# A layout planner's table of costs, its thresholds per visit, and the order in which waits are listed

## The chip, the cores and the metric

The kernel runs on one core of one Trainium2 chip. The time is the device time of one launch in microseconds; for the kernel before it is the median of three runs. A profile of one further execution is shown; its times are that execution's own.

## The reference

Two attention blocks over the same input `x` (1 x 2048 x 640, 32 heads of 20) are mixed by a gate of one number per token. Block A is full softmax attention; block B looks at 8 earlier positions, two apart.

```python
def _A_ref(x, wqkv, wo):
    q, k, v = ...                       # x @ wqkv, 32 heads of 20
    p = _softmax(jnp.einsum("bhqd,bhkd->bhqk", q, k) * scale, axis=-1)
    o = jnp.einsum("bhqk,bhkd->bhqd", p, v)
    return o.reshape(B, S, D) @ wo

def _B_ref(x, wqkv, wo):
    W, dil = 8, 2
    idx = pos[:, None] - (jnp.arange(W) * dil)[None, :]
    logits = jnp.einsum("bhsd,bhswd->bhsw", q, kg) * scale   # masked where idx < 0
    o = jnp.einsum("bhsw,bhswd->bhsd", _softmax(logits), vg)
    return o.reshape(B, S, D) @ wo

g = _sigmoid((x * gate_w).sum(-1, keepdims=True))
return g * a + (1 - g) * b              # a = _A_ref(x, ...), b = _B_ref(x, ...)
```

Nearly all of the work is block A's: 32 heads x 2048 x 2048 scores, each through an exponential.

## The kernel before

**Units and tiles.** Block A's scores are cut into units: one head, 128 keys, 512 queries. There are 2048 units, in 32 groups (a quarter of the queries and four heads each; `GROUPS`). A *tile* `s` (a *visit* of the main loop) takes two or three units. `qk(s)` (L1511) issues one matmul per unit into one of two PSUM buffers `score[s % 2]` (L1524), `exp(s)` (L1544) is one ScalarE activation over all of the tile's columns into one of five buffers `ebuf[s % 5]` (L1547), and `pv_slot` with `pv` (L1556) accumulates the products with the values in `obank`, four heads side by side (L1592). A score buffer has room for three units, and its third bank also serves as one of the three side banks `BANKS`.

**Rides.** A two-unit tile may carry a third unit that ScalarE doesn't touch. Its scores go to the third bank, VectorE turns them into `uD` (L1537) by integer arithmetic on the bits of a bf16 number, and three more VectorE operations with added shifts make `eD` (L806). The exponential of that unit is then the weighted sum of these four approximations, taken by four accumulations into `obank`, the weights being in `vS` (L798, on GpSimd). Four rides share their keys and form a quad; an `eD` operation covers the quad at once.

**Side work.** Everything else is written as Python generators: the projections of q, k and v (`gen_qd`, `gen_kd`, `gen_v`), the gate (`gen_gate`), block B (`gen_bproj`, `gen_b`), the normalisation of a finished group (`gen_norm`), the output projection (`gen_fold`, `gen_prefold`). A generator yields a request such as `("pe", cost, ready)`, `("dve", ahead, ready)`, `("act", ready)` or `("bank",)`, and goes on to issue its tasks when `step` (L1150) grants it.

**The planner.** No order of instructions is written by hand but for the head (to the first tile) and the tail (after the last). While the program is being built, `_Sched.task` (L188) books each instruction on its engine: it starts when its engine is free and when each task it depends on has ended plus a latency (`LAT`), and lasts for a charged duration. `SWITCH` is charged on TensorE whenever row-tiled matmuls (scores) follow column-tiled ones or the reverse. From these booked times the loop at the end of `_build` decides, visit by visit, how the next tile is formed (`next_tile`, `wanted`), which accumulations go in (`pv_slot`), and how much side work may be issued before the next tile (`spend`, up to the end of the previous exponential plus `SLACK`). `filler` (L1599) adds matmuls that change nothing where TensorE's booked load over the last 2.3 us is under `FILL`. The times decide only the order within each engine's queue; on the chip, semaphores decide when things run.

**Thresholds.** `PLAN` maps a visit number to eighteen thresholds: two slacks, the tolerances for a third unit and for a ride (`XTOL`, `DWAIT`, `DIDLE`, `DIDLE2`, `DTIME`), priorities of rides and of block B, how far VectorE work is booked ahead (`DVE_AHEAD`, `DAHEAD`), boosts, `RFILL`, `FILL`, `HOLD` and `BOFF`. They hold until the next entry.

**Waits.** `emit` (L245) writes each engine's queue. In front of an instruction it lists one `wait_ge` per semaphore still to be waited for, in the order in which the awaited tasks were issued. As the program is built, the wait listed first is carried by the instruction itself; further ones stand ahead of it as semaphore instructions. An exponential from the sixth tile on has two: the older exponential that wrote the same `ebuf`, and its own score matmuls.

Of the kernel before, what the change touches and what calls it, by code (L numbers as in the profile page):

```python
# [5 lines left out]
FP32 = mybir.dt.float32  # L6
# [20 lines left out]
PADB = 16  # L27
SCALE = float(DH) ** -0.5
NEG = -1.0e9
TOK = 256  # L30
# [20 lines left out]
    0: ((0.3, 0.64), 0.31, 2.5, 2.5, 0.49, -1.34, -0.1, 11.8, 7.0, 8.15, 0.52, 0.47, 4.4, 4.0, 0.0, 0.71, 2, 0.0),  # L51
    10: ((0.3, 0.64), 0.31, 2.5, 2.5, 0.66, -1.34, -0.1, 11.8, 7.0, 8.15, 0.52, 0.47, 4.4, 4.0, 0.0, 0.71, 2, 0.0),
    20: ((0.3, 0.64), 0.31, 2.5, 2.5, 0.49, -1.34, -0.83, 11.8, 7.0, 8.15, 0.52, 0.47, 4.4, 4.08, 0.0, 0.71, 2, 0.0),
    30: ((0.32, 0.68), 0.31, 2.5, 5.5, 0.94, -1.34, -0.83, 11.8, 7.0, 7.65, 0.52, 0.47, 4.4, 5.28, 0.0, 0.73, 2, 0.0),
    40: ((0.32, 0.68), 0.3, 2.5, 5.5, 0.94, -1.34, -0.83, 11.8, 7.0, 8.82, 0.52, 0.47, 4.4, 5.28, 0.0, 0.73, 2, 1),
    50: ((0.32, 0.81), 0.3, 2.5, 5.5, 0.94, -1.34, -0.83, 11.8, 7.0, 8.82, 0.52, 0.47, 4.4, 5.28, 0.0, 0.73, 2, 1),
    60: ((0.32, 0.68), 0.31, 2.5, 5.5, 0.94, -1.34, -0.83, 11.8, 6.7, 7.65, 0.52, 0.64, 4.4, 4.34, 0.0, 0.73, 2, 0),
    70: ((0.32, 0.68), 0.3, 2.5, 5.5, 0.94, -1.5, -0.83, 11.8, 5.5, 8.82, 0.52, 0.47, 4.76, 5.28, 0.0, 0.73, 2, 1),
    80: ((0.29, 0.82), 0.3, 2.5, 5.5, 0.94, -1.34, -0.83, 11.8, 7.0, 8.82, 0.52, 0.47, 4.4, 5.28, 0.0, 0.73, 2, 1),
    90: ((0.29, 0.82), 0.06, 2.5, 6.6, 0.95, -1.34, -0.83, 11.59, 7.0, 8.82, 0.52, 0.47, 4.4, 5.28, 0.0, 0.73, 2, 0),  # L60
    100: ((0.32, 0.68), 0.31, 2.5, 5.5, 0.94, -1.34, -0.83, 11.8, 7.0, 7.03, 0.52, 0.47, 4.4, 4.3, 0.0, 0.69, 2, -3),
    110: ((0.32, 0.68), 0.31, 2.5, 5.5, 0.94, -1.49, -0.5, 11.8, 7.0, 6.64, 0.52, 0.47, 4.4, 4.3, 0.0, 0.66, 2, -3),
    120: ((0.32, 0.68), 0.31, 5.5, 5.5, 0.94, -1.15, -0.5, 9.67, 7.0, 6.64, 0.52, 0.47, 4.4, 3.98, 0.0, 0.66, 2, -3),
    130: ((0.32, 0.68), 0.31, 2.5, 5.5, 0.82, -1.6, -0.5, 11.8, 7.0, 6.64, 0.52, 0.44, 4.4, 4.54, 0.0, 0.66, 2, 0),
    160: ((0.31, 0.76), 0.33, 2.5, 1.0, 0.82, -1.6, -0.34, 11.8, 7.0, 6.64, 0.61, 0.44, 4.4, 4.12, 0.0, 0.66, 2, 0),
    180: ((0.31, 0.76), 0.28, 2.5, 1.0, 0.72, -1.6, -0.5, 11.8, 5.5, 6.64, 0.52, 0.44, 4.4, 3.94, 0.0, 0.66, 2, 0),
    190: ((0.31, 0.76), 0.28, 2.5, 5.5, 0.72, -1.6, -0.5, 11.8, 5.5, 6.64, 0.52, 0.59, 3.16, 3.94, 0.0, 0.66, 2, 0),
    200: ((0.32, 0.68), 0.38, 2.5, 2.5, 0.94, -1.48, -0.65, 14.9, 7.0, 6.07, 0.52, 0.47, 4.4, 5.28, 0.0, 0.73, 1, -3),
    210: ((0.29, 0.69), 0.31, 2.5, 5.5, 0.94, -1.49, -0.5, 11.8, 7.0, 7.54, 0.67, 0.62, 4.4, 4.3, 0.0, 0.66, 1, -3),
    230: ((0.29, 0.69), 0.38, 2.5, 5.5, 0.94, -1.49, -0.5, 11.8, 7.0, 7.54, 0.67, 0.51, 4.4, 4.3, 0.0, 0.8, 2, -3),  # L70
    240: ((0.29, 0.69), 0.19, 2.5, 5.5, 1.12, -1.49, -0.5, 11.8, 7.0, 7.54, 0.7, 0.55, 4.4, 3.84, 0.0, 0.7, 2, -3),
    250: ((0.29, 0.69), 0.28, 2.5, 5.5, 0.94, -1.49, -0.5, 11.8, 7.0, 7.54, 0.67, 0.62, 3.7, 4.3, 0.0, 0.69, 2, -3),
    260: ((0.36, 0.63), 0.38, 2.5, 2.5, 1.09, -1.48, -0.65, 9.61, 7.0, 6.07, 0.52, 0.47, 4.4, 5.28, 0.0, 0.73, 1, -3),
    270: ((0.29, 0.69), 0.24, 2.5, 5.5, 0.94, -1.29, -0.5, 11.74, 7.0, 7.54, 0.67, 0.62, 3.7, 4.3, 0.0, 0.72, 2, -3),
    300: ((0.29, 0.69), 0.24, 2.5, 5.5, 0.94, -1.29, -0.33, 11.74, 7.0, 7.54, 0.67, 0.62, 3.7, 4.3, 0.0, 0.72, 2, -3),
    310: ((0.29, 0.69), 0.27, 1.0, 6.6, 0.94, -1.6, 0.4, 11.8, 5.5, 6.93, 0.67, 0.54, 4.85, 4.42, 0.0, 0.66, 1, -3),
    320: ((0.29, 0.69), 0.27, 1.0, 6.6, 0.94, -1.5, 0.17, 9.99, 7.0, 8.58, 0.67, 0.54, 4.85, 5.04, 0.0, 0.66, 1, -3),
    330: ((0.37, 0.63), 0.24, 1.0, 5.5, 0.94, -1.29, -0.5, 11.74, 7.0, 7.54, 0.67, 0.62, 3.7, 4.3, 0.0, 0.71, 2, -3),
    340: ((0.29, 0.69), 0.16, 2.5, 2.5, 0.94, -1.37, 0.35, 12.91, 7.0, 7.54, 0.6, 0.62, 5.69, 4.65, 0.0, 0.72, 2, -3),
    360: ((0.29, 0.69), 0.32, 2.5, 5.5, 0.94, -1.25, 0.28, 11.3, 6.7, 7.78, 0.6, 0.62, 4.87, 3.21, 0.0, 0.72, 2, -3),  # L80
    380: ((0.29, 0.69), 0.24, 2.5, 1.0, 0.94, -1.29, 0.35, 11.3, 7.0, 9.58, 0.43, 0.43, 4.87, 4.3, 0.0, 0.72, 2, -3),
    390: ((0.29, 0.69), 0.24, 2.5, 5.5, 0.94, -1.29, 0.35, 11.3, 7.0, 9.58, 0.6, 0.62, 4.87, 4.37, -0.24, 0.84, 2, -3),
    400: ((0.32, 0.66), 0.25, 2.5, 2.5, 0.94, -1.37, 0.35, 12.77, 7.0, 6.11, 0.6, 0.62, 5.69, 4.87, 0.0, 0.72, 1, -3),
    410: ((0.3, 0.61), 0.25, 1.0, 2.5, 0.94, -1.38, 0.35, 12.77, 7.0, 6.11, 0.6, 0.62, 5.69, 4.87, 0.0, 0.72, 1, -3),
    420: ((0.34, 0.65), 0.25, 2.5, 2.5, 0.94, -1.37, 0.35, 12.67, 7.0, 7.4, 0.6, 0.62, 5.69, 4.3, 0.0, 0.73, 1, -3),
    430: ((0.32, 0.66), 0.25, 2.5, 2.5, 0.94, -1.41, 0.35, 10.51, 5.5, 7.99, 0.6, 0.62, 5.69, 4.87, 0.12, 0.72, 1, -3),
    440: ((0.32, 0.66), 0.25, 2.5, 2.5, 0.94, -1.37, 0.4, 13.22, 7.0, 7.57, 0.6, 0.62, 5.69, 3.69, 0.0, 0.72, 1, -3),
    450: ((0.3, 0.63), 0.25, 2.5, 2.5, 0.94, -1.37, 0.26, 7.4, 5.5, 6.11, 0.6, 0.67, 5.56, 5.42, -0.14, 0.61, 1, -3),
    490: ((0.28, 0.56), 0.25, 2.5, 6.6, 0.94, -1.46, 0.26, 7.4, 5.5, 6.11, 0.6, 0.73, 5.84, 5.55, -0.14, 0.61, 2, -3),
    500: ((0.3, 0.63), 0.25, 2.5, 6.6, 0.94, -1.46, 0.26, 7.4, 5.5, 6.11, 0.6, 0.62, 5.84, 4.93, -0.14, 0.61, 1, -1.5),  # L90
    510: ((0.3, 0.63), 0.24, 5.5, 6.6, 0.94, -1.37, 0.4, 7.8, 5.5, 6.29, 0.6, 0.67, 5.56, 5.93, -0.02, 0.6, 1, -3),
    530: ((0.3, 0.63), 0.07, 2.5, 2.5, 0.94, -1.06, 0.05, 7.4, 5.5, 8.96, 0.6, 0.67, 4.4, 5.42, -0.14, 0.61, 1, -1.5),
    540: ((0.34, 0.55), 0.35, 1.0, 6.6, 1.32, -1.37, 0.36, 13.82, 7.0, 10.51, 0.58, 0.73, 6.26, 4.87, -0.08, 0.65, 2, -3),
    550: ((0.34, 0.55), 0.35, 1.0, 6.6, 1.32, -1.37, -0.85, 13.82, 7.0, 10.51, 0.27, 0.73, 6.26, 5.26, -0.08, 0.65, 1, -3),
    560: ((0.3, 0.63), 0.07, 2.5, 2.5, 1.39, -1.06, 0.05, 7.4, 5.5, 8.96, 0.6, 0.67, 4.4, 5.42, -0.14, 0.69, 1, -3),
    570: ((0.3, 0.63), 0.07, 2.5, 2.5, 1.39, -1.06, 0.05, 7.4, 5.5, 8.84, 0.6, 0.67, 4.4, 5.42, -0.14, 0.69, 1, -3),
    580: ((0.33, 0.51), 0.25, 1.0, 5.5, 0.87, -1.26, -0.43, 13.15, 7.0, 7.41, 0.7, 0.51, 6.5, 4.87, -0.17, 0.67, 1, -3),
    590: ((0.33, 0.51), 0.25, 1.0, 5.5, 0.84, -1.37, -0.5, 12.77, 7.0, 7.41, 0.58, 0.51, 6.31, 4.87, -0.17, 0.67, 1, -3),
    600: ((0.33, 0.51), 0.25, 1.0, 5.5, 0.84, -1.37, -0.5, 12.77, 7.0, 7.41, 0.58, 0.51, 6.31, 4.87, -0.17, 0.67, 1, 1),
    620: ((0.3, 0.64), 0.32, 2.5, 2.5, 0.49, -1.0, 0.02, 11.8, 7.0, 7.2, 0.52, 0.47, 4.4, 4.0, 0.0, 0.85, 2, 0),  # L100
    630: ((0.33, 0.51), 0.25, 1.0, 5.5, 0.84, -1.47, -0.5, 12.41, 7.0, 7.41, 0.58, 0.51, 6.31, 4.87, -0.1, 0.67, 1, 1),
    640: ((0.3, 0.64), 0.32, 2.5, 1.0, 0.49, -0.36, -0.1, 11.8, 7.0, 11.41, 0.52, 0.47, 4.4, 4.0, -0.11, 0.6, 2, -3),
    650: ((0.33, 0.51), 0.25, 5.5, 5.5, 0.84, -1.37, -0.5, 12.77, 7.0, 7.41, 0.58, 0.45, 6.31, 4.87, -0.22, 0.67, 1, 1),
    680: ((0.33, 0.51), 0.25, 5.5, 5.5, 0.84, -1.37, -0.5, 12.77, 7.0, 7.41, 0.58, 0.45, 6.31, 4.24, -0.28, 0.67, 1, 1),
    690: ((0.37, 0.55), 0.24, 5.5, 2.5, 0.84, -1.37, -0.01, 12.77, 7.0, 7.41, 0.58, 0.45, 6.31, 4.87, -0.22, 0.67, 1, 0),
    700: ((0.33, 0.51), 0.25, 5.5, 5.5, 0.92, -1.32, -0.5, 12.77, 7.0, 7.41, 0.58, 0.45, 6.23, 4.15, -0.22, 0.67, 1, 1),
    710: ((0.37, 0.45), 0.22, 6.3, 6.6, 0.84, -1.37, -0.88, 12.77, 6.2, 7.19, 0.58, 0.46, 6.31, 4.87, -0.22, 0.65, 1, 1),
    720: ((0.46, 0.47), 0.22, 6.3, 6.6, -0.02, -1.37, -0.88, 12.77, 5.5, 7.19, 0.58, 0.46, 6.31, 4.87, -0.22, 0.65, 1, 0),
}
WEIGHTS = (1.0, 0.83984375, 0.70703125, 0.59375)  # L110
UOFF = 15992.765
K = len(SHIFTS)

LAT = {"pe": 0.22, "act": 0.18, "dve": 0.13, "pool": 0.15, "sp": 0.1}
SWITCH = 0.11
# [19 lines left out]
class _Sched:  # L137
# [23 lines left out]
    def ready(self, *keys):  # L161
        t = 0.0
# [6 lines left out]
    def free(self, *keys):  # L169
        t = 0.0  # L170
# [1616 lines left out]
```

## Time and profile before

| what | value |
|---|---|
| runs (three) | 832.91, 833.99, 834.21 us; median 833.99 |
| profiled execution: span from first to last instruction | 830.2 us |
| stretch before the first score exponential | 0 to 19.09 us |
| DVE, uD (L1537) | 324 operations, 684 ns each |
| DVE, eD (L806) | 243 operations, 725 ns each |
| PE, score matmuls (L1524) | 2048 |
| PE, accumulations (L1592) from ebuf / eD / uD | 1724 / 972 / 324 |
| PE, filler matmuls (L1613) | 296 + 140 + 100 |
| POOL | 139.1 us busy in 194 instructions |

The engines are PE (TensorE), PEld (its weight loads), DVE (VectorE), ACT (ScalarE), POOL (GpSimd) and SP, which issues DMAs. A group's row names the source line, the operation, its output and inputs, the shapes and the count, then the busy time, the mean length of one, and the idle time of the engine just before such instructions with what ended it. The reported length of an ACT or DVE instruction runs into the next one's, so lengths don't add up to time. A timeline row has start, length and, in brackets, the idle time before it; `x8` means that eight instructions of a kind were merged.

### The profile page before, as it was taken

How to read it: one execution, taken by the hardware profiler on the slowest of the kernel's cores; microseconds unless marked ns; L12 is line 12 of the kernel's file. 1: busy time of each engine (PE TensorE's matmuls, PEld its weight loads, DVE VectorE, ACT ScalarE, POOL GpSimd, SP SyncE). 2: the span in 40 equal slices, each digit the busy share in tenths (PEclk: the TensorE clock that was granted, in tenths of full speed). 3: DMA queues.
4: the chain of work that ended last, by engine and by line, in shares of the span. 5: the costliest groups of instructions: out<-in, count | busy, mean ns of one | idle time of the engine just before them, and what ended most of it. 6: DMA issues, size and time to landing. Idle time of an engine off the chain costs nothing.

```text
span 830.2 us, 29189 instructions
## 1 busy us (share of the span) xinstructions
PE 776.4 (94%) x12389; PEld 284.4 (34%) x12389; DVE 679.5 (82%) x1191; ACT 802.8 (97%) x763; POOL 139.1 (17%) x194
## 2 busy tenths in 40 slices
PE   8999999998999899999999998899999999998898
PEld 5332232333333332333244233333333433343223
DVE  7667787789989878887898988898887977889973
ACT  4999999999999999999999999999999999999995
POOL 5022111620211111021201011111011111101110
PEclk9999999999999999999999999999999999999999
DMA  9112210200111010011001011100111011100001
GB/s 310 35 36 47 47 35 19 71 21 15 36 34 31 24 29 20 7 40 34 18 18 44 19 20 41 31 22 7 34 30 27 6 39 33 33 7 21 21 6 34
DMA packets 45014, 29.12 MB, mean 35 GB/s; under 512 B 27204, under 2 KB 43684, under 8 KB 44884
## 3 DMA queue, kind: packets, MB, share of 16 engines
q1 hardware_dynamic: 44596, 26.92, 12.5%
q8 instruction: 98, 1.61, 0.8%
q10 hardware_dynamic: 288, 0.33, 0.1%
q14 instruction: 32, 0.26, 0.1%
HBM read 11.94 MB, written 2.62 MB: 18 GB/s over the span
## 4 chain that ended last, share of the span: by engine, by line
ACT 49%; PE 34%; issue 13%; DVE 4%; DVEq 0%; ACTq 0%
ACT ebuf L1547 49%; PE score L1524 10%; PE obank L1592 8%; PE side L566 8%; PE score L566 4%; DVE uD L1537 1%; DVE eD L806 1%; PE obank L468 1%; PE score L1239 1%; PE obank L1613 1%; ACT eB L923 0%; PE side L1262 0%; PE score L1613 0%; ACT tB L957 0%; PE score L693 0%
## 5 line engine op out<-in xcount | busy, mean ns | idle before, releaser
L1547 ACT ACTIVATE ebuf<-score 128x1024 bf16<-128x1024 f32 (+1 forms) x731 | 791.4, 1232 | 8.8 <-PE score L1524 6.7
L1524 PE MATMUL score<-qT,kT 32*128 32x512 bf16 x2048 | 290.9, 383 | 35.9 <-ACT ebuf L1547 24.3
L1537 DVE TENSOR_SCALAR uD<-score 128x512 int16<-128x512 f32 x324 | 217.1, 684 | 41.6 <-PE score L1524 38.9
L806 DVE TENSOR_SCALAR eD<-uD 128x2048 int16<-128x2048 int16 x243 | 169.0, 725 | 5.8 <-PE obank L1592 5.2
L1524 PEld LDWEIGHTS score<-qT,kT 32*128 32x128 bf16 x2048 | 74.9, 91 | 281.7 <-ACT ebuf L1547 121.0
L1592 PE MATMUL obank<-ebuf,vA 128*21 128x512 bf16 x1724 | 160.3, 385 | 2.6 <-ACT ebuf L1547 1.9
L798 POOL TENSOR_TENSOR vS<-vA,vw 128x252 bf16<-128x252 bf16 x81 | 60.2, 744 | 317.0 <-PE obank L1592 283.7
L566 PE MATMUL side<-xT,kvw 128*32 128x256 bf16 (+1 forms) x2540 | 102.6, 280 | 2.1 <-DVE qkvB L862 1.0
L1592 PE MATMUL obank<-eD,vS 128*21 128x512 bf16 x972 | 83.4, 379 | 0.3 <-DVE eD L806 0.3
L566 PEld LDWEIGHTS side<-xT,kvw 128*32 128x32 bf16 x2540 | 59.6, 96 | 34.8 <-issue 19.0
L1592 PEld LDWEIGHTS obank<-ebuf,vA 128*21 128x21 bf16 x1724 | 38.0, 89 | 87.7 <-issue 74.6
L773 POOL TENSOR_TENSOR rcp<-rcp,gA 128x16 f32<-128x16 f32 x31 | 8.7, 282 | 280.2 <-DVE rcp L771 280.2
L979 DVE TENSOR_TENSOR stage<-qkvB,repB 128x1280 bf16<-128x1280 bf16 x64 | 52.9, 852 | 0.0
L878 DVE TENSOR_TENSOR stage<-qkvB 128x1280 bf16<-128x1280 bf16 x64 | 52.6, 850 | 0.2
L862 DVE CAST qkvB<-side 128x512 bf16<-128x512 f32 (+1 forms) x72 | 42.0, 593 | 9.3 <-PE side L566 9.0
L566 PE MATMUL side<-stage,ident 128*32 128x512 bf16 (+1 forms) x736 | 47.9, 349 | 1.7 <-DVE oB L996 0.9
L779 POOL TENSOR_TENSOR oN<-oTt,rcp 128x512 bf16<-128x512 f32 x31 | 32.9, 1062 | 2.4
L767 DVE STREAM_TRANSPOSE oTt<-obank 128x512 f32<-128x512 f32 x32 | 22.8, 712 | 11.2 <-PE obank L1592 10.7
L1592 PE MATMUL obank<-uD,vA 128*21 128x512 bf16 x324 | 31.5, 379 | 0.0
L1592 PEld LDWEIGHTS obank<-eD,vS 128*21 128x21 bf16 x972 | 23.5, 91 | 16.2 <-issue 2.5
L1613 PE MATMUL obank<-xT,zero 128*32 128x512 bf16 x296 | 26.6, 384 | 0.0
L566 PE MATMUL side<-woA_d,oTd 128*32 128x512 bf16 (+2 forms) x520 | 26.0, 295 | 0.0
(169 smaller groups left out, 542.0 us busy)
## 6 DMA issues: line engine op xcount, KB each, us to landing
repB<-eB SPq DMA_DIRECT2D x128, 32.0 KB
WqP<-in_A_wqkv_dram SPq DMA_DIRECT2D x16, 160.0 KB
stage<-in_B_wqkv_dram SPq DMA_DIRECT2D x1, 2400.0 KB
oTd<-oN SPq DMA_DIRECT2D x108, 20.0 KB
qT<-dst SPq DMA_DIRECT2D x104, 20.0 KB
out_dram<-outsb SPq DMA_DIRECT2D x12, 160.0 KB
kvw<-in_A_wqkv_dram SPq DMA_DIRECT2D x2, 800.0 KB
oTd<-in_A_x_dram SPq DMA_DIRECT2D x2, 640.0 KB
```

Of the source, the lines that this page charges most:

```text
L566: ins = e.matmul(o[j:k, :], l(j) if callable(l) else l[:, j:k], r, start=(first and i == 0), stop=(last and i == n - 1), skip_group_check= ...
L779: T(en, c2, lambda e: e.tensor_tensor(oo, ii, ib, ALU.mult), reads=["rcp", "oTt"], writes=["oN0"])
L798: T("pool", 0.7, lambda e: e.tensor_tensor(vS[:, d % 2, :, :], _ap(vA, (kb * NQ + q) * 4 * DV, [[0, K - 1], [1, 4 * DV]]), _ap(vw, 0, [[1, ...
L806: T("dve", 0.11 + 0.1334 * n, lambda e, k=k, sl=sl: e.tensor_scalar(eD[:, sl % NS, 0:512 * n].bitcast(I16), uD[d % 2][:, 0:512 * n].bitcas ...
L862: t = TB(dvc(n * TOK), lambda e, o=o, i=i: e.tensor_copy(o, i), reads=[("side", b)], writes=[key])
L878: TB(dvc(CN * TOK, 2), lambda e, w=w, ks=ks: e.tensor_tensor(prodB(w), qB[:, :, :], ks, ALU.mult), reads=["qB", "kB"], writes=[("prod", w) ...
L979: TB(dvc(CN * TOK, 2), lambda e, w=w, vs=vs, rr=rr: e.tensor_tensor(prodB(w), vs, rr, ALU.mult), reads=["vB", ("repB", w4 % NR)], writes=[ ...
L1524: ins = e.matmul(o, kT[32 * j:32 * j + 32, q, kb * P:(kb + 1) * P], qT[g % NQT][32 * j:32 * j + 32, :], start=True, stop=True)
L1537: t = T("dve", 0.69, lambda e: e.tensor_scalar(uD[d % 2][:, 512 * i:512 * (i + 1)].bitcast(I16), side[x], UOFF, 0.0, op0=ALU.add, op1=ALU. ...
L1547: exps[s] = T("act", actc(512 * n), lambda e: e.activation(ebuf[s % NE][:, 0:512 * n], score[s % 2][:, 0:512 * n], ACTF.Exp, scale=LN2 / S ...
L1592: ins = e.matmul(obank[32 * j:32 * j + DV, :], v, src, start=(kb == 0), stop=(last and k >= len(lst) - 4), skip_group_check=True)
L1613: ins = e.matmul(o[32 * j:32 * j + 32, :], w[:, 32 * j:32 * j + 32] if best else w[:, :], xT[:, 0, 0:512], start=bool(best), stop=bool(bes ...
```

## The change

It touches the planner's table, its thresholds, and `emit`. No operation is added to or taken from the computation as such; the numbers of rides, of tiles and of fillers, and the order in each queue, come out of the planner.

1. *Charges.* The latency may now depend on both engines (`PAIR`, with `LAT` for the rest), the fixed part of a VectorE, ScalarE and matmul charge is changed, and single operations get their own charge. A score group is charged by the most units that fall on one row tile, an accumulation group 0.2225 for each four less 0.01. GpSimd is booked free 0.05 before its task ends. A wait for a DMA adds 0.1.
2. *Thresholds.* `PLAN` has new entries, now at multiples of five visits. Most rows are combinations like those of before.
3. *Waits.* They are listed by the booked end of the awaited task plus latency, latest first.

```diff
 PLAN = {
-    0: ((0.3, 0.64), 0.31, 2.5, 2.5, 0.49, -1.34, -0.1, 11.8, 7.0, 8.15, 0.52, 0.47, 4.4, 4.0, 0.0, 0.71, 2, 0.0),
-    10: ((0.3, 0.64), 0.31, 2.5, 2.5, 0.66, -1.34, -0.1, 11.8, 7.0, 8.15, 0.52, 0.47, 4.4, 4.0, 0.0, 0.71, 2, 0.0),
...
+    0: ((0.3, 0.64), 0.31, 1.0, 2.5, 0.49, -1.34, -0.1, 11.8, 7.0, 6.03, 0.52, 0.47, 4.4, 4.0, 0.0, 0.71, 3, -1.5),
+    5: ((0.38, 0.64), 0.31, 2.5, 2.5, 0.49, -1.34, -0.1, 11.8, 7.0, 7.68, 0.52, 0.47, 4.4, 4.0, 0.17, 0.71, 2, 0.0),
...
+    210: ((0.29, 0.69), 0.38, 2.5, 5.5, 0.94, -1.48, 1.19, 11.8, 7.0, 7.54, 0.52, 0.55, 4.4, 3.84, 0.0, 1, 1, -3),
...
+    615: ((0.34, 0.51), 0.25, 1.0, 5.5, 0.82, -1.26, -0.43, 13.15, 7.0, 7.41, 0.7, 0.51, 6.5, 4.81, 0.08, 0.2, 1, -3),
...
+    730: ((0.46, 0.47), 0.22, 6.3, 6.6, -0.02, -1.37, -0.88, 12.77, 5.5, 7.19, 0.58, 0.46, 6.31, 4.87, -0.22, 0.65, 1, 0),
 }
...
-LAT = {"pe": 0.22, "act": 0.18, "dve": 0.13, "pool": 0.15, "sp": 0.1}
-SWITCH = 0.11
+LAT = {"pe": 0.275, "act": 0.152, "dve": 0.083, "pool": 0.065, "sp": 0.1}
+PAIR = {("pe", "dve"): 0.215, ("pe", "pool"): 0.25, ("pe", "sp"): 0.25, ("act", "dve"): 0.17, ("act", "sp"): 0.17,
+        ("dve", "dve"): 0.127, ("dve", "act"): 0.124, ("dve", "pool"): 0.155, ("dve", "sp"): 0.13, ("pool", "dve"): 0.105,
+        ("pool", "pool"): 0.078, ("pool", "act"): 0.105}
+SWITCH = 0.105
+def lat(t, to):
+    return LAT[t.stream] if t.dom == "dma" else PAIR.get((t.stream, to), LAT[t.stream])
...
-            start = max(start, d.end + LAT[d.stream])
+            start = max(start, d.end + (0.1 if d.dom == "dma" else lat(d, stream)))
...
-                        for d in sorted(t.deps, key=lambda x: x.idx):
+                        for d in sorted(t.deps, key=lambda x: -x.end - lat(x, sname)):
...
-    mmc = lambda n: max(n, 64) / 2400.0 + 0.004
-    dvc = lambda n, mode=1: 0.10 + n * 1.0417e-3 / mode
-    actc = lambda n: 0.08 + n * 0.8334e-3
+    mmc = lambda n: max(n, 64) / 2400.0 + (0.0035 if n > 128 else 0.0035)
+    dvc = lambda n, mode=1: 0.064 + n * 1.0417e-3 / mode
+    actc = lambda n: 0.0635 + n * 0.8334e-3
...
-            T("dve", 0.11 + 0.1334 * n, lambda e, k=k, sl=sl: e.tensor_scalar(
+            T("dve", 0.065 + 0.1334 * n, lambda e, k=k, sl=sl: e.tensor_scalar(
...
-            T("pe", 0.12, fn, reads=["gwT"] + XT(qc), mode="col", **{"accum" if c else "writes": [("side", b)]})
+            T("pe", 0.031, fn, reads=["gwT"] + XT(qc), mode="col", **{"accum" if c else "writes": [("side", b)]})
...
-        T("pe", 0.24, fn, reads=["eB", "Rep"], mode="col", accum=[("side", b)])
+        T("pe", 0.068, fn, reads=["eB", "Rep"], mode="col", accum=[("side", b)])
...
-        t = T("pe", 0.215, fn, reads=sorted(rd, key=str),
+        t = T("pe", 0.2155 * max(js.count(j) for j in js), fn, reads=sorted(rd, key=str),
...
-            run_dve(t.end + LAT["pe"] - RFILL)
-            t = T("dve", 0.69, lambda e: e.tensor_scalar(
+            run_dve(t.end + PAIR["pe", "dve"] - RFILL)
+            t = T("dve", 0.598, lambda e: e.tensor_scalar(
...
-        T("pe", 0.215 * ((len(lst) + 3) // 4), fn, reads=sorted(rd, key=str), accum=["obank"], mode="col")
+        T("pe", 0.2225 * ((len(lst) + 3) // 4) - (0.01 if len(lst) > 4 else 0.0), fn, reads=sorted(rd, key=str), accum=["obank"], mode="col")
```

## The prediction

> **What bounds the kernel now.** I read the page first: span and busy shares, then the chain that ended last.
>
> ```profile
> span 830.2 us, 29189 instructions
> PE 776.4 (94%) x12389; PEld 284.4 (34%) x12389; DVE 679.5 (82%) x1191; ACT 802.8 (97%) x763; POOL 139.1 (17%) x194
> ...
> ACT 49%; PE 34%; issue 13%; DVE 4%; DVEq 0%; ACTq 0%
> ```
>
> ACT is busy almost throughout, but a third of the chain runs over PE: at many tiles the exponential was released by a matmul. To price this I took the groups with shapes kept apart.
>
> ```profile
> L1547 ACT ACTIVATE ebuf<-score 128x1024 bf16<-128x1024 f32 x469 | 452.5, 1074 | 5.0 <-PE score L1524 3.4 <-ACT ebuf L1547 0.2
> L1547 ACT ACTIVATE ebuf<-score 128x1536 bf16<-128x1536 f32 x262 | 367.5, 1513 | 3.8 <-PE score L1524 3.3
> ...
> L1537 DVE TENSOR_SCALAR uD<-score 128x512 int16<-128x512 f32 x324 | 217.1, 684 | 41.6 <-PE score L1524 38.9
> L806 DVE TENSOR_SCALAR eD<-uD 128x2048 int16<-128x2048 int16 x243 | 169.0, 725 | 5.8 <-PE obank L1592 5.2
> ```
>
> There are 731 tiles; 324 units of 512 columns "ride" on DVE instead of ACT. The means overlap from one instruction to the next, so they can't be added up. The step from start to start can be read in the timeline of ACT, in two undisturbed runs (first and a later start of each):
>
> ```profile
> 70.66 8.36 ACT L1547 ACTIVATE ebuf<-score 128x1024 bf16<-128x1024 f32 x9
> ...
> 77.91 2.03 ACT L1547 ACTIVATE ebuf<-score 128x1024 bf16<-128x1024 f32 x2
> ...
> 648.10 13.58 ACT L1547 ACTIVATE ebuf<-score 128x1536 bf16<-128x1536 f32 x10
> ...
> 660.10 2.93 ACT L1547 ACTIVATE ebuf<-score 128x1536 bf16<-128x1536 f32 x2
> ```
>
> Eight steps of the small tile take 7.25 us, 0.906 each; nine of the large one 12.00 us, 1.333 each. So the exponentials need 469 x 0.906 + 262 x 1.333 = 424.9 + 349.2 = 774.1 us, and the eight eB exponentials and small tanh calls some 7 more (eB: 8 x 0.712 = 5.7 busy). The first exponential starts at 19.09, the last ends at 816.94 + 2.37 = 819.3: a window of 800.2. **About 19 us of it are bubbles**, mostly too short to count as idle because the tail of the instruction before covers them. The other way down is fewer columns on ACT.
>
> **The change, part by part.**
>
> The computation and each operation's size stay; what moves is how many units ride, and where side work is put between tiles. DMAs keep their number and sizes (their share is 0.05 to 0.18 in every 80 us window after the first 20 us), only SP's order shifts with its producers: I cost that at nothing, covered by the depth of the buffers; if a load came late, the wait would stand as DMA before a score matmul, and none stands among the longest waits now. The head, 19.09 us, and the tail, 830.2 - 819.3 = 10.9 us, are placed by hand; 0.5 us either way.
>
> *1. Charges and thresholds: rides.* What DVE really takes, from its timeline:
>
> ```profile
> 409.02 1.29 DVE L806 TENSOR_SCALAR eD<-uD 128x2048 int16<-128x2048 int16 x2
> 410.23 0.68 DVE L1537 TENSOR_SCALAR uD<-score 128x512 int16<-128x512 f32 x1
> 410.83 0.68 DVE L806 TENSOR_SCALAR eD<-uD 128x2048 int16<-128x2048 int16 x1
> 411.79 0.69 DVE L1537 TENSOR_SCALAR uD<-score 128x512 int16<-128x512 f32 x1 [0.27 <-PE score L1524]
> 413.81 0.69 DVE L1537 TENSOR_SCALAR uD<-score 128x512 int16<-128x512 f32 x1 [1.33 <-PE score L1524]
> ```
>
> Two eD step over 1.21 us, one uD over 0.60. The old table charges 0.69 for a uD and 0.644 for a four-unit eD, the new one 0.598 and 0.599; the new figures are those of the trace. Over the program the old table overcharged DVE by 324 x 0.092 + 243 x 0.045 + 624 others x 0.036 = 29.8 + 10.9 + 22.5 = 63 us. The planner opens a ride when DVE, by its own sum, is soon free, so it refused rides that DVE had room for: the last two lines show it idle before uD, 1.33 us once.
>
> A ride costs DVE 0.60 + 3/4 x 0.60 = 1.05 us, PE three more accumulations (about 3 x 0.215/4 = 0.16), and takes 1.333 - 0.906 = 0.427 off ACT. Upper end: all 63 us spent on rides, 60 of them, -25.6 us. Lower end: the new thresholds hold rides back (one row of the new table goes to 1.19 where the old stood at -0.5), say ten fewer, +4.3. Between them I go by windows of 80 us (busy PE, PEld, DVE, ACT, POOL):
>
> ```profile
> 20.00:100.00 80.00, 78.61 (x1141) 25.80 (x1137) 54.59 (x115) 76.88 (x79) 12.55 (x14) 1.00 0.18 44
> ...
> 420.00:500.00 80.00, 76.67 (x1320) 29.29 (x1317) 71.17 (x122) 79.87 (x76) 10.65 (x16) 1.00 0.11 25
> ...
> 660.00:740.00 80.00, 76.18 (x1282) 27.43 (x1278) 62.71 (x111) 79.69 (x75) 11.86 (x19) 1.00 0.11 29
> ```
>
> DVE reached 71.2 in the fullest window. Lifting the eight windows from 100 to 740 to that adds 4.5 + 1.1 + 1.7 + 4.6 + 0 + 0.3 + 4.8 + 8.5 = 25.5 us, 24 rides. Rides come in fours and need a free score bank, so I take 20: **-8.6 us**. PE's extra 20 x 0.16 = 3.2 us is covered by its fillers (L1613: 536 matmuls, 134 groups of 0.215 = 29 us); without that cover it would be +3.2.
>
> *2. Wait order.* An exponential waits for its score matmuls and, from the sixth tile on, for an older exponential too; the old order lists the older first. Three releases:
>
> ```profile
> 18.65 0.39 PE L1524 MATMUL score<-qT,kT 32*128 32x512 bf16 x3 [0.33 <-DVE qT L1346]
> ...
> 19.09 1.45 ACT L1547 ACTIVATE ebuf<-score 128x1536 bf16<-128x1536 f32 x1 [2.19 <-PE score L1524]
> ...
> 186.35 0.60 PE L1524 MATMUL score<-qT,kT 32*128 32x512 bf16 x3
> ...
> 186.99 0.69 DVE L1537 TENSOR_SCALAR uD<-score 128x512 int16<-128x512 f32 x1 [0.31 <-PE score L1524]
> 187.05 1.02 ACT L1547 ACTIVATE ebuf<-score 128x1024 bf16<-128x1024 f32 x1 [0.26 <-PE score L1524]
> ```
>
> The first tile has one wait and starts 0.05 us after the matmul's end (18.65 + 0.39 = 19.04). At 187 the same matmul (end 186.95) releases DVE after 0.04 and ACT after 0.10. I read this as 0.06 us lost where the late wait isn't the one that the instruction itself carries.
>
> [...]
>
> Behind a held exponential stand the next ones, and behind these PE's accumulations. Both ends: 731 tiles x 0.06 = 44 us is more than the bubbles hold, so at most -19; if the order works the wrong way, +0.06 at the 11 visible stalls, +0.7.
>
> *3. Closer latencies.* PE to ACT is now charged 0.275 (was 0.22), a mode switch 0.105 (0.11), so side groups end earlier before a tile. This too only acts on the 19 us, with the same ends. For parts 2 and 3 together I take a third of the bubbles, **-6 us**: the nearer row is the 6.7 us that ACT is seen idle behind PE.
>
> The clock could speak against it: the page shows it at 9 in every slice and the window rows at 1.00. [...]
>
> **Sum**: -8.6 - 6 = -14.6 on the profiled span of 830.2 gives 815.6. The runs' median of 833.99 lies 3.8 above the span; with that margin unchanged, **819.4 us**.
>
> **Rivals.**
>
> *A, PE comes late (slower).* The new table charges small matmul groups far less (0.12 to 0.031, 0.24 to 0.068), so more is packed ahead of each score group, and PE is in order. It decides from 14.6/731 = 0.020 us of added lateness per tile; at 0.030 the loss is 21.9 - 14.6 = +7.3: 841. For it: PE is busy 78.6 of 80 us in the first window. Against: PEld 34%, 29 us of fillers.
>
> *B, rides don't grow.* The score bank, not DVE's charge, limits them: 262 tiles use it for a third unit and 324 for a ride, 80% of 731. Only part 2 and 3 remain: 828.
>
> *C, the room is used fully.* 50 rides and the 6 us: -21.4 - 6 = 806.6. Against: 53 us more DVE work would put the windows over 75 of 80.
>
> *D, it does not do what it says*: the rows are a reshuffle, gains and losses cancel: 834.
>
> **How the numbers follow.** Forecast (813 to 825) 0.50, B 0.17, C 0.12, A 0.15, D 0.06. The range reaches into C below and A above: 806 to 838. From no change a measurement here tells about 0.2%, 1.7 us. Faster: 0.50 + 0.17 + 0.12 = 0.79; the same 0.06; slower 0.15.
>
> **What would show it.** Rides: uD of L1537 near 344 instead of 324, large plus small tiles still near 731. Wait order: starts 0.04 to 0.05 after the matmul on ACT late in the run too. Bubbles: window less steps near 13. A: more idle on ACT behind PE, over 9 us. It would be wrong if uD stays at 324, or if the window's steps leave more than 19 us.

## The result, and the profile after

The changed kernel takes **822.87 us** (median of four runs, 820.86 to 824.32) against 833.98 beside it: ratio 0.9871, 95% interval 0.9856 to 0.9886. The forecast was 819.4, in a range of 806 to 838. The direction and the sum hold, the sum by luck: its terms don't, and the runs below take it apart.

The page of the changed kernel first: span, busy shares, and the shares of the chain that ended last.

```profile
span 821.3 us, 29318 instructions
PE 771.7 (94%) x12399; PEld 280.8 (34%) x12401; DVE 718.2 (87%) x1261; ACT 784.6 (96%) x752; POOL 148.0 (18%) x204
...
PE 37%; ACT 31%; DVE 17%; issue 14%; POOL 0%; ACTq 0%; DVEq 0%
```

ACT lost 18 us of work, DVE gained 39, and the chain is now spread over three engines where ACT had half of it. The groups with shapes apart say how (uD is now L1582, eD L850, the exponential L1592):

```profile
L1592 ACT ACTIVATE ebuf<-score 128x1024 bf16<-128x1024 f32 x474 | 458.6, 1099 | 5.5 <-PE score L1568 4.3
L1592 ACT ACTIVATE ebuf<-score 128x1536 bf16<-128x1536 f32 x245 | 346.8, 1530 | 3.7 <-PE score L1568 3.4
...
L1582 DVE TENSOR_SCALAR uD<-score 128x512 int16<-128x512 f32 x364 | 240.4, 678 | 20.6 <-PE score L1568 19.3
L850 DVE TENSOR_SCALAR eD<-uD 128x2048 int16<-128x2048 int16 x273 | 192.9, 729 | 2.5 <-PE obank L1637 1.7
```

364 rides instead of 324. The windows of 80 us (busy PE, PEld, DVE, ACT, POOL, then clock) show where DVE took them (two last columns: DMA share, GB/s):

```profile
20.00:100.00 80.00, 77.38 (x1130) 25.05 (x1122) 58.74 (x121) 77.25 (x76) 12.98 (x14) 1.00 0.16 38
...
500.00:580.00 80.00, 74.76 (x1243) 26.59 (x1235) 77.78 (x134) 79.57 (x77) 14.71 (x20) 1.00 0.09 24
...
660.00:740.00 80.00, 74.27 (x1235) 27.39 (x1228) 75.00 (x127) 78.40 (x73) 13.46 (x20) 0.98 0.09 23
```

DVE is now busy up to 77.8 of 80, past the 71.2 that was its fullest window before.

**Where the time went** is read from three points: the start of the first exponential, the end of the last, and the end of the span. The last exponentials and what ACT does next, in the kernel before, and then the first and last exponentials in the changed one (before, the first starts at 19.09):

```profile
816.94 2.37 ACT L1547 ACTIVATE ebuf<-score 128x1536 bf16<-128x1536 f32 x2 [0.16 <-PE score L1524]
825.50 1.08 ACT L1091 ACTIVATE stage<-score 128x512 bf16<-128x512 f32 x2 [6.20 <-PE score L1072]
```

```profile
18.82 1.45 ACT L1592 ACTIVATE ebuf<-score 128x1536 bf16<-128x1536 f32 x1 [2.09 <-PE score L1568]
...
795.33 5.98 ACT L1592 ACTIVATE ebuf<-score 128x1536 bf16<-128x1536 f32 x5
816.20 0.60 ACT L1135 ACTIVATE stage<-side 128x512 bf16<-128x512 f32 x1 [14.90 <-PE side L1116]
```

The last exponential ends at 801.3, 18 us earlier than before (819.3). Then ACT waits 14.9 us, where it waited 6.2. Half of what the exponentials gained is given back behind them.

The same accounting for every run: *own* is what the tiles need at 0.906 us for two units and 1.333 for three, as worked out in the prediction; *bubbles* are the window from first to last exponential less own and 7 us of small activations; *tail* is from the last exponential to the end of the span. All are of one profiled execution each; of the same program twice (`after`, `after_again`) the bubbles differ by 2.4, of which a drop of the clock, told at the end, makes 1.3; a smaller difference in bubbles between two rows says nothing. `thin_b7` leaves out a part of block B, as told below.

| run | median, us | ratio to before (95%) | rides | window | own | bubbles | tail |
|---|---|---|---|---|---|---|---|
| before | 833.98 | | 324 | 800.2 | 774.1 | 19.1 | 10.9 |
| after | 822.87 | 0.9871 (0.9856 to 0.9886) | 364 | 782.5 | 756.5 | 19.0 | 20.0 |
| wait_only | 827.25 | 0.9934 (0.9921 to 0.9948) | 324 | 795.8 | 774.1 | 14.7 | 10.8 |
| wait_act | 829.51 | 0.9958 (0.9944 to 0.9971) | 324 | 797.3 | 774.1 | 16.2 | 10.8 |
| old_wait | 827.60 | 0.9935 (0.9923 to 0.9948) | 364 | 786.0 | 756.5 | 22.5 | 20.3 |
| costs_only | 855.76 | 1.0270 (1.0252 to 1.0289) | 340 | 818.7 | 767.3 | 44.4 | 17.9 |
| plan_only | 866.87 | 1.0407 (1.0392 to 1.0421) | 319 | 823.8 | 776.1 | 40.7 | 20.8 |
| ud_2ns | 841.63 | 1.0111 (1.0096 to 1.0126) | 340 | 802.5 | 767.2 | 28.3 | 18.5 |
| cut_672 | 826.01 | 0.9926 (0.9907 to 0.9946) | 348 | 786.6 | 763.3 | 16.3 | 17.9 |
| cut_632 | 830.54 | 0.9970 (0.9960 to 0.9979) | 320 | 800.4 | 775.2 | 18.2 | 9.4 |
| thin_b7 | 823.86 | 0.9905 (0.9883 to 0.9927) | 364 | 780.9 | 756.5 | 17.4 | 20.0 |
| searched | 821.80 | 0.9869 (0.9850 to 0.9889) | 368 | 777.9 | 754.9 | 16.0 | 21.3 |
| searched_tail | 820.77 | 0.9855 (0.9841 to 0.9868) | 368 | 781.5 | 754.9 | 19.6 | 20.0 |
| after_again | 822.88 | 0.9888 (0.9871 to 0.9905) | 364 | 780.1 | 756.5 | 16.6 | 20.2 |

From before to after: own -17.6, bubbles -0.1, tail +9.1, head -0.3; together -8.9, the difference of the spans (830.2 to 821.3). With the bubbles of `after_again`, 16.6, their term would be -2.5.

### The profile page after: what moved, and what is told of

It reads as the page before. It is cut to its first block, busy times and chain, and to the rows that moved or that the text cites. A ratio compares the mean times of both kernels' runs of the same rounds, so it can differ in the third digit from the quotient of the medians.

```text
span 821.3 us, 29318 instructions
## 1 busy us (share of the span) xinstructions
PE 771.7 (94%) x12399; PEld 280.8 (34%) x12401; DVE 718.2 (87%) x1261; ACT 784.6 (96%) x752; POOL 148.0 (18%) x204
## 4 chain that ended last, share of the span: by engine, by line
PE 37%; ACT 31%; DVE 17%; issue 14%; POOL 0%; ACTq 0%; DVEq 0%
ACT ebuf L1592 30%; PE score L1568 11%; PE obank L1637 9%; PE side L610 9%; DVE uD L1582 7%; DVE eD L850 4%; PE score L610 4%; PE obank L1658 1%; DVE qkvB L906 1%; DVE stage L1023 1%; PE obank L512 1%; DVE stage L922 1%; PE score L1283 1%; ACT eB L967 0%; DVE oB L1040 0%
## 5 line engine op out<-in xcount | busy, mean ns | idle before, releaser
L1592 ACT ACTIVATE ebuf<-score 128x1024 bf16<-128x1024 f32 (+1 forms) x720 | 773.2, 1245 | 9.2 <-PE score L1568 7.7
L1568 PE MATMUL score<-qT,kT 32*128 32x512 bf16 x2048 | 285.0, 385 | 29.2 <-ACT ebuf L1592 18.6
L1582 DVE TENSOR_SCALAR uD<-score 128x512 int16<-128x512 f32 x364 | 240.4, 678 | 20.6 <-PE score L1568 19.3
L850 DVE TENSOR_SCALAR eD<-uD 128x2048 int16<-128x2048 int16 x273 | 192.9, 729 | 2.5 <-PE obank L1637 1.7
L1568 PEld LDWEIGHTS score<-qT,kT 32*128 32x128 bf16 x2048 | 70.8, 91 | 267.4 <-ACT ebuf L1592 186.5
L1637 PE MATMUL obank<-ebuf,vA 128*21 128x512 bf16 x1684 | 156.8, 386 | 1.9 <-DVE eD L850 0.5
L842 POOL TENSOR_TENSOR vS<-vA,vw 128x252 bf16<-128x252 bf16 x91 | 66.7, 735 | 278.6 <-PE obank L1637 246.5
L1637 PE MATMUL obank<-eD,vS 128*21 128x512 bf16 x1092 | 95.9, 380 | 0.0
L1637 PE MATMUL obank<-uD,vA 128*21 128x512 bf16 x364 | 35.3, 379 | 0.0
L610 PE MATMUL side<-woBp,oB 128*32 128x512 bf16 (+1 forms) x500 | 24.9, 304 | 1.0 <-DVE qkvB L906 0.6
```

The source lines that it names most:

```text
L610: ins = e.matmul(o[j:k, :], l(j) if callable(l) else l[:, j:k], r, start=(first and i == 0), stop=(last and i == n - 1), skip_group_check= ...
L842: T("pool", 0.607, lambda e: e.tensor_tensor(vS[:, d % 2, :, :], _ap(vA, (kb * NQ + q) * 4 * DV, [[0, K - 1], [1, 4 * DV]]), _ap(vw, 0, [[ ...
L850: T("dve", 0.065 + 0.1334 * n, lambda e, k=k, sl=sl: e.tensor_scalar(eD[:, sl % NS, 0:512 * n].bitcast(I16), uD[d % 2][:, 0:512 * n].bitca ...
L1568: ins = e.matmul(o, kT[32 * j:32 * j + 32, q, kb * P:(kb + 1) * P], qT[g % NQT][32 * j:32 * j + 32, :], start=True, stop=True)
L1582: t = T("dve", 0.598, lambda e: e.tensor_scalar(uD[d % 2][:, 512 * i:512 * (i + 1)].bitcast(I16), side[x], UOFF, 0.0, op0=ALU.add, op1=ALU ...
L1592: exps[s] = T("act", actc(512 * n), lambda e: e.activation(ebuf[s % NE][:, 0:512 * n], score[s % 2][:, 0:512 * n], ACTF.Exp, scale=LN2 / S ...
```

## The experiments

**The order of the waits alone**, in the kernel before, on all engines and then on ScalarE's queue only.

```diff
-                        for d in sorted(t.deps, key=lambda x: x.idx):
+                        for d in sorted(t.deps, key=lambda x: -x.end - LAT[x.stream]):                                # wait_only
+                        for d in sorted(t.deps, key=lambda x: -x.end - LAT[x.stream] if sname == "act" else x.idx):   # wait_act
```

> Before, with the latest wait listed first and nothing else changed (same order of instructions on every engine, 324 rides, 731 tiles). Theory: the late start of ACT, 0.107 us after a score matmul's end, becomes 0.047 at every held tile; about 115 tiles are held by more than 0.02 us, so 115 x 0.06 = 7 us at most and about 4 to go: 829 to 831. Rival, the bubbles are PE's and only shift: the same within 0.2%, 832.5 to 835.5. Rival, the wait that the instruction carries is not the one listed first: slower, over 836.

> Before, with the latest wait first on ScalarE's queue alone; TensorE, VectorE, GpSimd and SyncE keep the old order. Theory: the 0.06 us at the start of a held exponential make the whole gain of the order, so as with all engines, 826.5 to 828.5. Rival: TensorE's own waits for an exponential, which stood ahead of its matmuls, make most of it: 830 to 833.

`wait_only` gains 5.5 us, `wait_act` 3.1; `wait_only` is faster than even the theory had it. The layout is the same, and so is the number of semaphore instructions that stand ahead of others (751 on ScalarE's queue in both traces, 447 and 446 on TensorE's): this is the price of the order, not of fewer waits. The release that the prediction showed at 187 us, in `wait_only`:

```profile
184.99 0.60 PE L1524 MATMUL score<-qT,kT 32*128 32x512 bf16 x3
...
185.62 1.02 ACT L1547 ACTIVATE ebuf<-score 128x1024 bf16<-128x1024 f32 x1 [0.20 <-PE score L1524]
185.63 0.69 DVE L1537 TENSOR_SCALAR uD<-score 128x512 int16<-128x512 f32 x1 [0.38 <-PE score L1524]
```

The matmul ends at 185.59; ACT now starts with DVE, 0.03 to 0.04 later, where it started 0.06 behind it. Over all exponentials that ACT visibly waited for, the median from the matmul's end is 0.107 us before and 0.047 after. The rest of the gain is not ACT's. Who waited for the exponentials, in `before`, `wait_act` and `wait_only` (us, times):

```profile
  PEld score L1524: 121.0, 288
```

```profile
  PEld score L1524: 116.9, 279
```

```profile
  PEld score L1524: 202.8, 483
```

The time that PEld stood idle before score loads is the same in all three, 281.7, 279.7 and 281.9 us. What moves is what it is put down to: in `wait_only` less of it is "issue" (45.5 against 88.0), because the late wait is now on the weight load itself, where the profile sees it. A held score group's first weight load starts 0.04 to 0.06 us after an exponential's end 81 times in `before`, 75 in `wait_act`, 178 in `wait_only`, and 0.10 to 0.12 after it 150, 129 and 54 times. TensorE's own late waits had the same 0.06 us on them. Of my two expectations for `wait_act` neither held: by the medians ScalarE makes a little over half (0.42% of 0.66%), and the intervals leave that share wide.

**The new layout without the new order.**

```diff
-                        for d in sorted(t.deps, key=lambda x: -x.end - lat(x, sname)):
+                        for d in sorted(t.deps, key=lambda x: x.idx):
```

> The changed kernel with the waits in the old order of issue (same layout, 364 rides, 720 tiles). Theory: it loses what the order gave, 0.06 us at each held tile, and as the new layout was booked with shorter steps it loses at least as much as the other kernel won: 826 to 830. Rival, the order is worth nothing: 821 to 825.

827.60, as the theory had it: the order is worth 3.9 to 5.3 us here too (ratio 0.9935 against 0.9888 in `after_again` and 0.9871 in `after`), and the new layout with the old order 5.4 (0.65% of 833). Within these intervals the two parts of the change add up.

**Charges and thresholds apart.** `costs_only` has the old `PLAN` in the changed kernel, `plan_only` the new `PLAN` in the kernel before.

```diff
-PLAN = { ...the new rows... }
+PLAN = { ...the old rows... }          # costs_only; plan_only is the reverse, in the kernel before
```

> The changed kernel with the old table of thresholds: new charges, new wait order, 340 rides in 730 tiles. Theory, that the rides carry the gain as long as block B is done in time: 16 rides more than before, last score exponential some 16 x 0.427 = 7 us earlier than with 324, about 812 us into the span. The end is the question: if the old thresholds leave block B as unfinished as the new ones do, 9 us of that are lost in the tail and the time is near 834; if they leave it at the old tail, 826. Rival, the charges alone do it: 823.

> Before with the new table of thresholds: old charges, old wait order, 319 rides in 728 tiles. Theory: thresholds are good only with the charges that they were found with; 5 rides fewer and a layout of no search, so slower than before by 2 to 20 us, 836 to 854. Rival, the thresholds carry the gain whatever the charges: 823 to 828.

Both are far slower than before, 2.7% and 4.1%, and worse than every expectation (at most 834 and 854). Own time behaves as the rides say; what is new is 41 to 44 us of bubbles instead of 19. ACT stands visibly idle behind score matmuls for 27.5 us in `costs_only` and 26.0 in `plan_only`, against 6.7 before. The longest in `costs_only`:

```profile
67.49 4.35 SPq L720 DMA_DIRECT2D qT<-qbnd  x8
...
72.87 0.61 PE L1531 MATMUL score<-qT,kT 32*128 32x512 bf16 x3 [4.66 <-DMA qT<-qbnd]
...
73.53 1.02 ACT L1555 ACTIVATE ebuf<-score 128x1024 bf16<-128x1024 f32 x1 [4.67 <-PE score L1531]
```

The projection of the next group's q was placed so late that its eight DMAs were still being issued when the tile needed them. I had costed the DMAs' order at nothing, and named this as what a late load would look like; in `after` no such wait stands, in an unsuited layout it does. It cost more than its 4.66 us: in the windows from 70 to 74 and from 74 to 78 the granted clock was 0.53 and 0.62, and the four accumulations at 73.41 took 0.61 us, where four took 0.40 in the kernel before (at 403.19, clock 1.00). What makes the other bubbles of the two runs was not traced.

**How closely the thresholds hang on the charges.** One charge moved by 0.002 us:

```diff
-            t = T("dve", 0.598, lambda e: e.tensor_scalar(
+            t = T("dve", 0.600, lambda e: e.tensor_scalar(
```

> The changed kernel with one charge moved by 0.002 us: a uD is booked at 0.600 instead of 0.598; the planner then makes 340 rides in 729 tiles. Theory, that thresholds fit only the bookings they were found with and the gain is in their having been picked for exactly these: 20 to 35 us slower, 845 to 858. Rival, that the closeness of the charges to the trace makes the gain: a charge two thousandths off is as close, so only the 24 rides fewer count, 10 us less what the tail gives back: 823 to 833.

841.63, 2.3% above `after`, between the two and nearer the first: 24 rides fewer (own +10.7) and 9 us more bubbles, 1.5 less tail. A charge as true to the trace as before, and the gain is gone and more. So closeness to the trace alone does not make the gain; the thresholds fit the very bookings that they were found with. This is one move of one charge: how often so small a move costs so much is not shown.

**What late rides are worth.** No new quad from visit 632, or 672, on:

```diff
         if not dopen:
+            if len(tiles) >= 632:
+                return None
             if ulock[len(dquads) % 2] or ...
```

> The changed kernel, but no new quad of rides is opened from visit 632 on: 320 rides instead of 364, the layout up to that visit unchanged. Theory: each ride is worth 0.427 us of ACT, so the last exponential ends 44 x 0.427 = 19 us later, near 820 us of the span; in exchange VectorE is free for block B, which ends in time, and the tail falls from 20.0 to the old 11: net 9 to 10 us slower, 831 to 834. Rival, the tail does not depend on the rides: 841. Rival, late rides cost as much as they give: 821 to 825.

> The same from visit 672 on: 348 rides. Theory: last exponential 16 x 0.427 = 7 us later, the tail shorter by some 2 to 4 us: 826 to 829. Rival, tail independent of rides: 830; rival, late rides are worth nothing: 821 to 825.

Both fell where the theory had them or within 0.5 us. With 320 rides the last exponential ends at 819.01 and the tail is short again:

```profile
815.30 3.71 ACT L1594 ACTIVATE ebuf<-score 128x1536 bf16<-128x1536 f32 x3
823.21 0.60 ACT L1135 ACTIVATE stage<-side 128x512 bf16<-128x512 f32 x1 [4.19 <-PE side L1116]
```

44 rides fewer cost 18.7 us of own time and bring 10.6 back in the tail. So the late rides lengthen it, and what stands in it is work of block B. In `after`, behind the last exponential:

```profile
801.79 1.90 PE L610 MATMUL side<-stage,ident 128*32 128x512 bf16 x32
...
803.52 1.90 PE L610 MATMUL score<-stage,ident 128*32 128x512 bf16 x32
...
804.43 0.65 DVE L1040 SCALAR_TENSOR_TENSOR oB<-side,rB 128x512 bf16<-128x512 f32 x1
...
806.83 0.46 PE L610 MATMUL score<-woBp,oB 128*32 128x128 bf16 x20 [0.53 <-DVE oB L1040]
...
810.76 1.26 PE L610 MATMUL side<-woBp,oB 128*32 128x512 bf16 x20
...
815.53 0.41 PE L1116 MATMUL score<-outsb,oN 128*32 128x128 bf16 x16
```

The sums over block B's last 256 tokens, its scaling, then the last column block of the output projection: in the kernel before all this lay between tiles, and only what starts here at 810.76 came after. Over all fourteen runs the tail goes with this: where block B's last scaling starts ahead of the last exponential's end (by 8.7 us in `cut_632`, by 17.3 to 17.4 in `before`, `wait_only` and `wait_act`), the tail is 9.4 to 10.9 us; in the other ten it starts 3.7 to 6.6 behind, and the tail is 17.9 to 21.3.

What holds block B up is open. The expectations had it that the rides leave VectorE no time for it, and in `after` VectorE is busy for 75.0 of 80 us from 660 to 740. But `plan_only` has 319 rides and a tail of 20.8, and in `cut_672` block B's last part comes late though VectorE has room; its scaling there waits for PE's sums. Windows of `after`, `cut_632` and `cut_672` (busy PE, PEld, DVE, ACT, POOL, clock), and the scaling in `cut_672`, whose last exponential ends at 806.1:

```profile
740.00:800.00 60.00, 57.70 (x930) 19.92 (x929) 50.96 (x87) 59.80 (x57) 7.37 (x11) 1.00 0.08 23
...
740.00:800.00 60.00, 50.38 (x866) 19.32 (x867) 22.87 (x41) 60.00 (x48) 2.91 (x5) 1.00 0.08 23
...
740.00:800.00 60.00, 54.63 (x904) 19.38 (x894) 32.52 (x57) 59.91 (x52) 5.13 (x7) 1.00 0.08 23
...
805.80 0.69 DVE L1040 SCALAR_TENSOR_TENSOR oB<-side,rB 128x512 bf16<-128x512 f32 x1 [3.32 <-PE side L610]
```

VectorE is busy 51.0 of 60 us in the first and 32.5 in the last. Whether PE, a side bank that a ride occupies or the planner's order holds block B up, no run separates.

**Is that sum on the tail's path?** Same layout, the sum shrunk: for block B's last tokens six of its eight terms are left out but for 64 columns.

```diff
+            if u == 2 * QCN - 1:
+                mms[1:7] = [(side[b][:, 0:64], ident[:, :], _ap(stage, (w * CN + f0) * TOK, [[1, 64]]))
+                            for w in (4, 1, 5, 2, 6, 3)]
```

> The changed kernel with the same layout; the accumulation of block B's last 256 tokens, which now runs after the last exponential, is left out but for 64 columns in six of its eight terms (18 of 24 matmul groups shrink). Theory: this accumulation stands on the path of the tail, so 12 x (0.215 - 0.031) + 6 x (0.11 - 0.031) = 2.7 us of PE go and the time falls by 2 to 3 us: 819.5 to 821. Rival, the tail hangs on the normalisation of the last group on VectorE: no change, 822 to 824.

No change, 823.86, with the tail at 20.0; the expectation failed. Windows of the tail, `after` and then `thin_b7` (busy PE, PEld, DVE, ACT, POOL, clock):

```profile
802.00:806.00 4.00, 4.00 (x92) 2.36 (x88) 3.45 (x7) 0.00 (x0) 0.00 (x0) 1.00 0.00 0
806.00:810.00 4.00, 3.05 (x148) 2.12 (x140) 0.59 (x2) 0.00 (x0) 0.00 (x0) 1.00 0.01 4
```

```profile
802.00:806.00 4.00, 1.54 (x79) 1.09 (x68) 3.04 (x7) 0.00 (x0) 0.00 (x0) 0.94 0.00 0
806.00:810.00 4.00, 4.00 (x140) 2.83 (x133) 0.08 (x1) 0.00 (x0) 0.00 (x0) 0.63 0.02 4
```

PE did fall idle, but block B's scaling stands on DVE behind the normalisation of the last group, so it started 3.1 us after the last exponential in both. In `thin_b7`, where the last exponential ends at 800.37:

```profile
803.47 0.65 DVE L1043 SCALAR_TENSOR_TENSOR oB<-side,rB 128x512 bf16<-128x512 f32 x1
...
805.29 0.55 PE L610 MATMUL score<-woBp,oB 128*32 128x128 bf16 x20 [0.53 <-DVE oB L1043]
...
809.80 1.26 PE L610 MATMUL side<-woBp,oB 128*32 128x512 bf16 x20
```

The projection starts 4.92 us after the last exponential instead of 5.52, a lead of 0.6 where 2.7 was expected. Behind the stretch in which PE was busy 1.54 of 4 us the clock fell to 0.63, and at the next column blocks (809.80 here, 810.76 in `after`, 9.43 and 9.46 us behind the last exponential) the lead is gone. The rival was right that the tail hangs on VectorE first; the small lead that was left went while the clock was low.

**Other thresholds late in the program, and the tail in another order.** New thresholds from visit 630 on in both, and in `searched_tail` also the last column block's part that doesn't need block B put first:

```diff
...
+                parts = [fold_mms(side[b][:, blk * P:(blk + 1) * P], blk, qs, 512, D, True) for blk in range(4)]
+                for m_ in parts:
+                    yield from mm_group(b, m_[CN:], rd[:NQ], mmc(128), last=False, per=3)
+                while not done.get(("b", 2 * QCN - 1)):
+                    yield ("cond",)
+                for m_ in parts:
+                    yield from mm_group(b, m_[:CN], rd[NQ:] + [("oB", 1, f0) for f0 in range(0, CN, 2)], mmc(128), first=False, per=3)
...
```

> The changed kernel with other thresholds from visit 630 on (368 rides, 721 tiles), found with the new charges. Theory: 4 more rides are worth 4 x 0.427 = 1.7 us of ACT, and the planner's own end moves by -2.0 us; if bookings carry over as they did so far, 820 to 822. Rival: gains of this size drown in bubbles that the planner does not book, 822 to 825.

> The same thresholds, and in the tail the half of the last column block of the output projection that does not need block B is put ahead of the half that does, so that PE has work while VectorE finishes block B (in the changed kernel PE stood 0.81 us before the one and 0.75 in the midst of it). Theory: 0.5 to 1.5 us less than the kernel beside it, 819 to 821. Rival: PE has as much to do after as before, no difference.

> The changed kernel once more beside these two, for the comparison on one chip: 821.5 to 824 by every theory.

`searched_tail` is the fastest, 820.77 (0.9855, 0.9841 to 0.9868) against 822.88 (0.9888, 0.9871 to 0.9905) for the changed kernel on the same chip, 0.3% less and only just clear of the noise. `searched` alone, 821.80, can't be told from either.

## Why the prediction came out as it did

*Rides (-8.6, measured -17.6).* The mechanism held, down to the 0.427 us: 40 rides times 0.427 is 17.1, and 11 tiles fewer give the rest. The size was off by a factor of two. The step that failed is "Lifting the eight windows from 100 to 740 to that": I took the fullest window of the old layout as DVE's limit, but that was the limit of a planner that overcharged DVE. Its true room was what the trace's steps left. The 40 rides lie midway between my middle of 20 and my upper end of 60.

*Wait order and latencies (-6, measured -0.1 net in `after`, -2.5 in `after_again`).* The order was read rightly from one pair of releases and is worth some 4 to 5.5 us in either layout. The 6 us for parts 2 and 3 together were nearly met by part 2 alone; but the denser layout seems to bring bubbles of its own (22.5 in `old_wait` against 19.1 before, hardly more than two executions differ by). My sign was bubbles near 13; at 19.0 `after` stands on the bound that I had set for being wrong. That closer latencies by themselves shorten bubbles is not shown by any run. The case that the order works the wrong way is out.

*Tail ("placed by hand; 0.5 us either way", measured +9.1).* This step was wrong. Only the tail's own instructions are placed by hand; what side work is left when the tiles end is the planner's, and here it left block B's last part. I had checked what a ride displaces on PE and not whether block B would still end in time. That late rides are a cause, `cut_632` shows; through which engine or bank, `cut_672` leaves open.

*The sum* was near by luck: the two large errors, 9.0 us too few from rides and 9.1 us of tail, cancel. The bubbles that stayed leave the span 5.7 us over the 815.6 of the forecast, and 2.2 of these go again in the margin from span to median, 3.8 before and 1.6 here.

*Margin.* The span fell by 8.9 and the median by 11.1: the profiled execution of `after` was the longest of its four (824.32 us; see the clock below). In `after_again` the span is 819.0 and that execution's time 821.05.

*Rival A* (PE late) did not come: ACT's visible idle time behind PE is 7.7 us against 6.7, under the 9 that was its sign, and the bubbles did not grow. *Rival B* (rides limited by the score bank) is refuted by 364 rides. *Rival C* was half right: its 50 rides were nearer to the 40 than my 20, and its time did not come. *Rival D* (no change) is refuted by the ratio, though part of what it said, gains and losses that cancel, is what the tail did to the rides.

## What to carry to other kernels

When work is taken off the bounding engine, follow the side work to the end of the program: what is left over comes out where nothing covers it any more, here in the tail. In a list of waits, let the instruction carry the one that comes last; here it cost nothing and gave 0.7% with no other change. And a planner that is tuned against its own bookings should be tuned again whenever a charge changes: here 2 ns on one charge undid the gain.

## What was not expected of the hardware

The clock. The same program, in `after` and in `after_again`, in the same stretch of the program (the exponential of tile 620 starts at 688.45 in the one and at 687.19 in the other, so the windows are taken 1.26 us apart):

```profile
687.50:691.50 4.00, 2.53 (x36) 0.83 (x36) 4.00 (x8) 4.00 (x5) 0.00 (x0) 1.00 0.12 30
691.50:695.50 4.00, 4.00 (x62) 1.68 (x58) 2.68 (x5) 3.09 (x4) 0.00 (x0) 0.58 0.04 11
```

```profile
686.24:690.24 4.00, 2.53 (x36) 0.83 (x36) 4.00 (x8) 4.00 (x5) 0.00 (x0) 1.00 0.12 29
690.24:694.24 4.00, 3.94 (x81) 1.66 (x77) 3.87 (x9) 4.00 (x5) 0.00 (x0) 1.00 0.05 12
```

In both executions PE was busy 2.53 of 4 us. In one the clock fell to 0.58 for the next window, and ACT lost 0.9 us there; in the other it stayed. From the exponential of tile 620 to that of tile 635 the one took 18.2 us and the other 16.9, so the drop cost 1.3 us. Seven profiled executions share this layout and this order of waits up to visit 630; the clock fell here in three (`after`, `cut_632`, `searched_tail`) and not in four (`after_again`, `cut_672`, `thin_b7`, `searched`). PE was not idle throughout the stretch; what makes the clock fall in one execution and not in another is not shown.

The prediction has no term for the clock. The lowest filler threshold of the new table, 0.2, holds for tiles 615 to 619, and these ran at full clock (1.00) in both executions; the drop follows tiles 620 to 623, where the threshold is 0.39. That the threshold is the cause was not tried. Drops that come in some runs and not in others would fit the wider spread of the changed kernel (3.5 us in four runs, 4.8 in five, against 2.3 to 2.6 in sets of nine to twelve of the kernel before).
